# Attention with a top-1 expert layer on one core: zero writes moved into the attention, and a re-drawn plan

## The chip, the cores and the metric

The kernel runs on one core of one Trainium2 chip. The time is the device time of one execution in microseconds (us). The kernel before was timed three times: 327.14, 327.40 and 329.66 us, with a median of 327.4 us. Lower is better. The core has a matrix engine (PE, with its weight loads shown as PEld), a vector engine (DVE), a scalar engine (ACT), GpSimd (POOL), and SyncE (SP), which here only issues transfers. The transfers themselves run on 16 DMA engines.

## The reference, cut to what matters

```python
# q, k, v: (8 batches, 8 heads, 576 positions, 64), float32
scores = scale * q @ k.T                      # heads 0-3: local mask, heads 4-7: strided mask
attn   = softmax(where(mask, scores, -1e9))
x      = (attn @ v) as 4608 tokens x 512
logits = x @ w_gate                           # 8 experts
expert_idx, gate_w = argmax and softmax value of the logits
out    = zeros(4608, 512)
for e in range(8):                            # w1[e]: 512 x 1024, w2[e]: 1024 x 512
    tok = the 80 (capacity) tokens of expert e with the largest gate_w
    out[tok] = gate_w[tok] * (relu(x[tok] @ w1[e]) @ w2[e])
```

At most 640 of the 4608 rows of `out` are not zero. All 9.4 MB of `out` must still be written with zeros, and all 33.5 MB of expert weights must be read.

## The kernel before, in words

**Three stages.** (1) The attention, batch by batch in 32 steps (four per batch: two for the local heads, two for the strided heads). Its result is turned into token rows that are written to a scratch tensor `xs` in HBM, and into logits and gates. (2) The routing: the largest 16 gates per segment, their ranks, the slot of every kept token, and a gather of the kept rows from `xs` (`gather`, L1070). (3) The experts: 16 halves (w1 or w2 of one expert), 96 matmuls of 128x80 each, and a scatter of 80 rows of `out` per expert (L1173).

**Weights.** A half is four chunks of 512 KB, so there are 64 chunks. `wload` (L260) puts a chunk into a staging slot. ACT or POOL makes the high fp16 part (`high`, L268 or L270), then DVE makes the low part (L757 in the attention, L278 behind it). In the attention there are two staging slots (`ring`). From chunk 20 on there are eight: the two of `ring`, four pieces of `raw` and two pieces of `kst`; `raw` and `kst` hold q, k and transposed k during the attention. Split halves lie in `spl`: five buffers in the attention, eight afterwards.

**Zeros.** `zero_out` (L777) writes 512 KB of zeros from a 128 x 256 piece of `raw` called `zt`, so a packet has 1024 bytes. There are 18 of these writes.

**What sets the order.** In the attention an operation is put into a list with a priority, an engine (or two to choose from), a cost and its dependencies (`Plan.add`). `Plan.order` then walks through a model of the machine: at each step it takes the operation that can start first, ties within `SLACK` go by priority, and for transfers it keeps the time at which the DMA engines will be free. The sorted start times are the program order on every engine, and engines execute in that order. Weights and zeros are `bg` operations: they are taken only when the modelled transfer backlog is below `BGT`. Zeros are also `drop`: what has not been placed when the last steps begin is issued behind the attention (`pl.dropped`, L980). `lag` marks operations that may fall behind the others. Behind the attention the order is written out by hand: `rows_left` copies the last token rows, and `weave` mixes the halves, the splits and the scatters.

**Transfers.** All of them but the gathers and scatters are issued on SP, in program order. Each also waits for the transfer that was issued eight places before it on SP, because there are eight completion semaphores (DMAHW0 to 7).

Of the kernel before, what the change touches and what calls it, by code (L numbers as in the profile page):

```python
# [20 lines left out]
P = 128  # L21
# [37 lines left out]
class Plan:  # L59
# [6 lines left out]
    def add(self, prio, eng, cost, fn, rd=(), wr=(), mode=None, take=(), size=0, bg=False, after=(), lag=False, drop=False):  # L66
# [18 lines left out]
        self.ops.append(o)  # L85

    def order(self):
# [3 lines left out]
        dma, mode, fills = 0.0, None, []  # L91
        users, cand = {}, {e: [] for e in free}
# [7 lines left out]
        for _ in self.ops:  # L100
# [26 lines left out]
            if e == "T" and t - free["T"] > FGAP and (t < FILL0 or low > FILL1):  # L127
                i = min((i for i in range(nb) if held[i] is None), key=lambda i: bt[i], default=None)
                if i is not None and bt[i] < t - FGAP:
                    f, m = Op(), int((t - max(free["T"], bt[i]) - FGAP / 2) / C_FILL)  # L130
                    f.start, f.on, f.seq, f.fn = max(free["T"], bt[i]), "T", o.seq, lambda e, i=i, m=m: self.filler(i, m)
                    f.mode, f.cost, f.deps, f.take, f.size = 128, m * C_FILL, [], (), 0
# [34 lines left out]
def moe_attention(ctx: ExitStack, tc, q, k, v, wg, w1, w2, cap, out):  # L167
# [50 lines left out]
    outv = out.rearrange("(g p r) (h f) -> g p (r h) f", p=P, r=2, h=2)  # L218
# [152 lines left out]

    def do_load(l):

        b, g, w = l // 4, l // 2 % 2, l % 2
        src, t = (q, k)[w], raws[l % 3]
# [7 lines left out]
        add(l - QAH, "S", C_DMA, fn, wr=[raw_(l % 3)], size=560)  # L383
# [14 lines left out]
    def do_transposes(l):  # L398
        g, w = l // 2 % 2, l % 2
        i = cps[w] if g == 0 else raws[l % 3].rearrange("p u f -> p (u f)").rearrange("p (j f) -> p j f", f=P)  # L400
# [8 lines left out]
        for j3 in range(3):  # L409
# [7 lines left out]
            add(pr, "T", C_TR * 3, fill, rd=[CPS[w][j3] if g == 0 else raw_(l % 3)], wr=[x], take=[x], mode=128,  # L417
                after=[((("qt", j3), ("qs", j3))[g]) if w == 0 else ((("ktl", u, j3), ("kst", u, j3))[g]) for u in range(len(dvs))])
            for u, d in enumerate(dvs):
# [3 lines left out]
                add(pr + E_EV, "AV", c_copy(384, 0.1), ev, rd=[x],  # L423
# [43 lines left out]
    def do_scores(j):  # L467
# [67 lines left out]
        add(pj(j) + E_SUM, "V", (0.66 if g == 0 else 0.9) + 1.07e-3 * nt * nk, total, rd=PN, wr=[("sm", j % NPB)])  # L535
# [14 lines left out]
    def do_values(j):  # L550
# [6 lines left out]
        if g == 0:  # L557
            t0 = TL[it][0]
            for a, (c0, c1) in enumerate(TG[it]):
# [7 lines left out]
                for u in range(2):  # L567
                    add(pj(j) + E_PT + E_EV, "AV", c_copy(P * n, -0.03), lambda e, x=x, c0=c0, c1=c1, n=n, u=u: copy(
# [20 lines left out]
        else:  # L589
# [12 lines left out]
            for z0 in (0, 2):  # L602
# [10 lines left out]
                add(pj(j) + E_PT + E_EV, "AV", dict(A=0.86, V=0.7), ev, rd=[x], wr=[("pts", z0)])  # L613
# [72 lines left out]
    def do_logits(b):  # L686
# [5 lines left out]
        add(pr + 0.3, "A", 0.41, lambda e: nc.scalar.copy(lt, cols(x, 288)), rd=[x], wr=["lt"])  # L692
# [53 lines left out]
    def do_weights(i):  # L746
# [3 lines left out]
        if i >= NCH * NPRE:  # L750
            nm = [[("ring", 0)], [("ring", 1)], [raw_(0)], KST, KST][i - NCH * NPRE]
        pr = W0 + i * WSTEP
        add(pr - WAH, "S", C_DMA, lambda e: wload(i), wr=nm, size=524, bg=True)
        if i < NCH * NPRE:
            sn = ("spl", i // NCH)
            add(pr, "PA", dict(P=1.1, A=1.06), lambda e: high(e, hi, r), rd=nm, wr=[("hi", i)], lag=True)
            add(pr + 0.2, "V", 1.35, lambda e: nc.vector.scalar_tensor_tensor(lo, r, SC, hi, op0=ALU.mult,  # L757
# [18 lines left out]
    def zero_out(nz):  # L776
        nc.sync.dma_start(outv[nz], zt.unsqueeze(1).broadcast_to([P, 4, 256]))  # L777

    def do_constants():
# [54 lines left out]
    for l in range(3):  # L834
        do_load(l)
    do_constants()
    nr = 0
    for i in range(n + 2):
        if i == 0:
            for l in range(2):  # L840
                do_interleave(l)
                do_transposes(l)
                do_load(l + 3)
# [38 lines left out]
        if i == n + 1:  # L882
# [3 lines left out]
            add(pj(n - 1) + 4.4, "V", 0.25, lambda e, x=x: nc.vector.tensor_copy(g288[:, 2], cols(x, NQ)), rd=[x])  # L886
# [11 lines left out]
    nc.vector.memset(zt, 0.0)  # L898
# [448 lines left out]
```

## Time and profile before

| | |
|---|---|
| median of 3 runs | 327.4 us |
| the profiled execution, its own time | 326.44 us |
| its span, first to last instruction | 324.7 us |
| attention, to about | 205 us |
| last token rows and routing, to the first transpose of gathered rows | 229.60 us |
| experts, to the last matmul of a half | about 317 us |
| last scatters, to the end | 324.7 us |
| busy: PE, DVE, ACT, POOL | 266.4, 232.6, 224.9, 143.2 us |
| moved by DMA | 84.27 MB, mean 260 GB/s |

The profile cuts the span into 40 slices of 8.1 us and gives the busy share of each engine in tenths. Its answers by stretch of time give busy microseconds, the granted PE clock, the busy share of the DMA engines (which reads a little above 1 when they are full, since packets overlap) and the GB/s moved. Behind the attention a matmul of 128x80 is shown with a duration near 200 ns, but such matmuls are pipelined: counting how many are in a stretch says more than their busy time.

### The profile page before, as it was taken

To read this page: it belongs to the slowest core of one execution; us is meant where nothing else is said; L and a number is where in the kernel's file an instruction comes from. 1 tells how busy PE (TensorE), PEld (TensorE's weight loads), DVE (VectorE), ACT (ScalarE), POOL (GpSimd) and SP (SyncE) were. 2 spreads that over 40 slices of the span, in tenths; PEclk is the share of its full clock that TensorE was granted. 3 is DMA by queue.
4 is the path that set the end of the run, shared out by engine and by line. 5 is a ranking of instruction groups with operands and counts; after the bars stand their busy time and mean duration, and the time that the engine had idled before them with its cause. 6 is when DMAs were issued, how large, how long until landed. Compare 5 with 4: busy or idle time off the path is not lost. (4 is left out here: it accounts for less than half of the span.)

```text
span 324.7 us, 12775 instructions
## 1 busy us (share of the span) xinstructions
PE 266.4 (82%) x5408; PEld 236.0 (73%) x5408; DVE 232.6 (72%) x481; ACT 224.9 (69%) x440; POOL 143.2 (44%) x161
## 2 busy tenths in 40 slices
PE   7889799998998869986979889995670798789791
PEld 7788588777877758875758667885570797789791
DVE  7647588988897974876988974397320998779860
ACT  1569479896887587987888957680310998779751
POOL 8569754961753760474673860054410061111002
PEclk9999799999999997999999999997596599999997
DMA  7998868899799985888985998499999999998701
GB/s 248 197 334 261 216 200 226 224 313 245 216 244 268 278 246 176 226 253 225 261 222 137 273 226 310 133 275 333 372 360 342 402 392 377 393 351 283 272 24 46
DMA packets 56433, 84.27 MB, mean 260 GB/s; under 512 B 23346, under 2 KB 32564, under 8 KB 56372
## 3 DMA queue, kind: packets, MB, share of 16 engines
q1 hardware_dynamic: 55348, 80.79, 82.3%
q0 software_dynamic: 1024, 2.62, 2.3%
q8 instruction: 44, 0.72, 0.9%
q14 instruction: 17, 0.14, 0.1%
HBM read 63.21 MB, written 20.19 MB: 257 GB/s over the span
## 5 line engine op out<-in xcount | busy, mean ns | idle before, releaser
L1128 PEld LDWEIGHTS <-spl 128*128 128x128 f16 x512 | 52.9, 103 | 13.9 <-issue 13.7
L1129 PEld LDWEIGHTS <-spl 128*128 128x128 f16 x512 | 52.8, 103 | 5.0 <-issue 5.0
L1127 PEld LDWEIGHTS <-spl 128*128 128x128 f16 x512 | 52.9, 103 | 3.1 <-issue 3.1
L536 POOL TENSOR_TENSOR pb<-pb,sm 128x288 f32<-128x288 f32 (+2 forms) x32 | 37.9, 1183 | 34.1 <-DVE sm L534 23.7
L444 POOL TENSOR_SCALAR vlo<-vlo 32x1152 f32<-32x1152 f32 (+1 forms) x32 | 37.9, 1183 | 9.4 <-DMA vlo<-v 6.3
L1127 PE MATMUL yp<-he,spl 128*128 128x80 f16 x256 | 31.2, 208 | 11.1 <-ACT he L1142 10.9
L278 DVE SCALAR_TENSOR_TENSOR spl<-raw,spl 128x1024 f16<-128x1024 f32 x21 | 25.3, 1219 | 17.3 <-ACT spl L268 17.2
L1127 PE MATMUL hp<-xe,spl 128*128 128x80 f16 x256 | 31.3, 206 | 3.7 <-issue 2.7
L1128 PE MATMUL yp<-he,spl 128*128 128x80 f16 x256 | 31.1, 208 | 2.5 <-issue 1.4
L1129 PE MATMUL hp<-xe,spl 128*128 128x80 f16 x256 | 31.2, 206 | 1.4 <-issue 1.4
L268 ACT ACTIVATE spl<-raw 128x1024 f16<-128x1024 f32 x21 | 21.7, 1052 | 15.1 <-DMA raw<-moe_w 15.1
L1129 PE MATMUL yp<-he,spl 128*128 128x80 f16 x256 | 31.1, 208 | 1.0 <-issue 1.0
L1128 PE MATMUL hp<-xe,spl 128*128 128x80 f16 x256 | 31.2, 206 | 0.5 <-DVE xe L1122 0.3
L1173 POOL DMA_INDIRECT out<-ys,ids x8 | 9.2, 1154 | 48.0 <-ACT ys L1172 40.9
L529 ACT ACTIVATE pb<-pb 128x288 f32<-128x288 f32 (+2 forms) x32 | 18.2, 569 | 16.3 <-DVE pb L522 16.2
L757 DVE SCALAR_TENSOR_TENSOR spl<-ring,spl 128x1024 f16<-128x1024 f32 x20 | 25.9, 1297 | 4.3 <-POOL spl L270 3.6
L343 ACT COPY ktl<-bank 64x384 f32<-64x384 f32 (+1 forms) x47 | 25.9, 567 | 3.8 <-DVE ktl L347 2.4
L520 DVE TENSOR_REDUCE mx<-bank 128x16 f32<-128x288 f32 (+3 forms) x40 | 20.1, 502 | 11.4 <-PE bank L514 6.5
L532 DVE TENSOR_REDUCE sm<-pb 128x16 f32<-128x288 f32 (+2 forms) x32 | 22.8, 713 | 5.2 <-ACT pb L529 5.1
L581 PE MATMUL bank<-ptl,vlo 128*64 128x64 f32 x576 | 21.5, 227 | 5.9 <-issue 5.0
L1070 POOL DMA_INDIRECT xg<-xs,idx x8 | 10.6, 1324 | 33.8 <-DMA raw<-moe_w 21.4
L611 ACT ACTIVATE pts<-bank,hm 72x288 f32<-72x288 f32 x52 | 22.1, 497 | 4.6 <-DVE pts L605 2.7
(205 smaller groups left out, 751.1 us busy)
## 6 DMA issues: line engine op xcount, KB each, us to landing
ring<-moe_w SPq DMA_DIRECT2D x32, 512.0 KB
raw<-moe_w SPq DMA_DIRECT2D x21, 512.0 KB
raw<-q SPq DMA_DIRECT2D x16, 576.0 KB
raw<-k SPq DMA_DIRECT2D x16, 576.0 KB
out<-raw SPq DMA_DIRECT2D x18, 512.0 KB
kst<-moe_w SPq DMA_DIRECT2D x11, 512.0 KB
xs<-xn SPq DMA_DIRECT2D x12, 384.0 KB
vs<-v SPq DMA_DIRECT2D x8, 512.0 KB
```

The costliest lines, as they stand in the source:

```text
L268: nc.scalar.activation(hi, r, AF.Copy, scale=SC)
L278: nc.vector.scalar_tensor_tensor(lo, r, SC, hi, op0=ALU.mult, op1=ALU.subtract)
L343: nc.scalar.copy(o, i)
L444: add(4 * b + m + 0.6 + 0.4 * u, "P", 1.25 if m == 0 else 1.1, lambda e: nc.gpsimd.tensor_scalar(vlo[64 * u:64 * u + 32, t0:t1], vlo[64 * ...
L532: nc.vector.tensor_reduce(each(sm[:, 0:nt], g), pq, op=ALU.add, axis=AX.X)
L536: add(pj(j) + E_MUL, "P", 0.2 + 1.7e-3 * nt * nk, lambda e: nc.gpsimd.tensor_tensor(plain(pa, g), plain(pa, g), spread(sm[:, 0:nt], g), op ...
L581: nc.tensor.matmul(o[64 * h:64 * h + 64, :, k0:k0 + 32], vlo[:, 2 * (t0 + c0 + c) + p, h], ptl[:, c0 + c, :, 32 * gg:32 * gg + 32], start= ...
L611: nc.scalar.activation(pts[:, z].rearrange("p g h c -> p (g h) c"), tv(x), AF.Copy, scale=hm[0:72, z:z + 1])
L757: add(pr + 0.2, "V", 1.35, lambda e: nc.vector.scalar_tensor_tensor(lo, r, SC, hi, op0=ALU.mult, op1=ALU.subtract), rd=nm + [("hi", i)], l ...
L1127: nc.tensor.matmul(o, w[:, 0, i:i + P], x[:, 0, c], start=first, stop=False)
L1128: nc.tensor.matmul(o, w[:, 0, i:i + P], x[:, 1, c], start=False, stop=False)
L1129: nc.tensor.matmul(o, w[:, 1, i:i + P], x[:, 0, c], start=False, stop=last)
```

## The change

The diff does five things.

1. **Zero writes.** The 18 writes of 512 KB become 9 writes of 1 MB. The source is a 64 x 1024 piece of the `kst` tile that is zero throughout the attention (the part of the block-diagonal k for the other half of the partitions). A packet has 4096 bytes, and the source has 64 partitions where it had 128. A load of weights into `kst` must wait for the write.
2. **The plan's model.** The transfer model gets a start latency (`DSTART`), a shorter end latency and a higher rate. Consumers of a transfer get a margin (`SMARGIN`, and `LMARGIN` for operations with `lag`), other operations a smaller one. Costs of copies and splits are changed. The backlog up to which background transfers are taken rises from 0.3 to 3 us.
3. **A drawn plan.** Each priority gets a random part below 0.3 from a fixed seed.
4. **The fourth load** (k of the strided heads of batch 0) goes to a buffer of its own (`xt`), so that it need not wait for a free piece of `raw`.
5. **Late operations.** Planned `lag` operations that start behind the last gates are issued behind the first part of the routing, together with the zeros that are left.

```diff
         dma, mode, fills = 0.0, None, []
+        rng = random.Random(SEED)
+        for o in self.ops:
+            o.prio += SPREAD * rng.random()
...
             if o.size:
-                dma = max(dma, t + c) + o.size / DRATE + DGAP
+                dma = max(dma + DGAP, t + c + DSTART) + o.size / DRATE
                 o.done = dma + DLAT
...
-                u.ready = max(u.ready, o.done + (0 if u.eng == e else MARGIN if u.eng == "T" else HOP))
+                m = 0 if u.eng == e else MARGIN if u.eng == "T" else HOP
+                if e == "S" and u.eng != e:
+                    m = LMARGIN if u.lag else SMARGIN
+                u.ready = max(u.ready, o.done + m)
...
-    outv = out.rearrange("(g p r) (h f) -> g p (r h) f", p=P, r=2, h=2)
+    outv = out.rearrange("(g p r c) f -> g p r (c f)", p=64, r=4, c=2)
...
-    zt = raw[:, 6 * S:6 * S + 256]
+    zt = kstt[0:64, 4 * S // 2:4 * S // 2 + 1024]
...
+    def raw_of(l):
+
+        if l == 3:
+            return xts_[0][1].rearrange("p (u f) -> p u f", u=2), [("xt", 0, 1, a) for a in range(4)]
+        return raws[l % 3], [raw_(l % 3)]
...
-            nm = [[("ring", 0)], [("ring", 1)], [raw_(0)], KST, KST][i - NCH * NPRE]
+            nm = [[("ring", 0)], [("ring", 1)], [raw_(0)], KST + ["kstz"], KST + ["kstz"]][i - NCH * NPRE]
...
     def zero_out(nz):
-        nc.sync.dma_start(outv[nz], zt.unsqueeze(1).broadcast_to([P, 4, 256]))
+        nc.sync.dma_start(outv[nz], zt.unsqueeze(1).broadcast_to([64, 4, 1024]))
...
-        for nz in range(18):
-            add(50 + nz, "S", C_DMA, lambda e, nz=nz: zero_out(nz), size=544, bg=True, drop=True)
+        for nz in range(9):
+            add(50 + nz, "S", C_DMA, lambda e, nz=nz: zero_out(nz), rd=["kstz"], size=1010, bg=True, drop=True)
...
+    late_ops = []
     for o in pl.order():
-        o.fn(o.on)
+        if o.start > final.start and o.lag:
+            late_ops.append(o)
+        else:
+            o.fn(o.on)
...
-    for o in pl.dropped:
-        o.fn("S")
+    for o in late_ops + pl.dropped:
+        o.fn(o.on)
...
-DRATE = 370.0
+DRATE = 390.0
-BGT = 0.3
+BGT = 3
```

In the program orders below a row is an instruction on one engine. `ring0` and `ring1` (121, 122), `raw` (123) and `kst` (124) are staging memory, `spl_129` is the fifth half of the split weights.

**SP at the end of the attention and behind it.** Before, the transfers of token rows (L724) are followed by 16 zero writes (L777) and then by loads of weights (L260):

```order
L724 DMA xs<-vlo 96x1024 x2
L724 DMA xs<-ktl 96x1024 x2
L777 DMA out<-raw 512x1x256 x16
L260 DMA raw<-moe_w 128x2x512 x3
L260 DMA ring_121<-moe_w 128x1024
L260 DMA ring_122<-moe_w 128x1024
```

In the changed kernel the same place reads (L741 token rows, L794 zeros, L270 weights):

```order
L741 DMA xs<-vlo 96x1024 x2
L741 DMA xs<-ktl 96x1024 x2
L270 DMA ring_122<-moe_w 128x1024
L794 DMA out<-kst 256x1x1024
L270 DMA kst<-moe_w 128x1024
L270 DMA kst<-moe_w 128x2x512
L270 DMA raw<-moe_w 128x2x512 x3
L270 DMA ring_121<-moe_w 128x1024
```

One zero write is left there instead of 16. Three loads of weights that stood ahead of the last rows or among them (chunks 21, 23 and 24) now stand behind them.

**SP in the last quarter of the attention.** Before, the first of two zero writes here (L777) stands among loads of v (L432) and of weights (L260):

```order
L260 DMA ring_121<-moe_w 128x2x512
L432 DMA vlo<-v 32x10x64 x2
L777 DMA out<-raw 512x1x256
L432 DMA vlo<-v 32x10x64 x2
L432 DMA vlo<-v 32x8x64 x2
L260 DMA ring_122<-moe_w 128x2x512
```

In the changed kernel four zero writes stand in this quarter, the first two of them (L794) one load of v (L449) apart:

```order
L455 DMA vs<-v 64x4x512
L794 DMA out<-kst 256x1x1024
L449 DMA vlo<-v 32x10x64
L794 DMA out<-kst 256x1x1024
L449 DMA vlo<-v 32x10x64
L270 DMA ring_122<-moe_w 128x1024
L449 DMA vlo<-v 32x8x64
```

The kernel before has two smaller ones in that quarter and none earlier; the changed kernel has four more earlier, the first behind the first two loads of weights.

**DVE at the beginning of the routing.** Before, the ranks (L1015, L1017) follow directly on the indices of the largest gates (L975, L976):

```order
L968 TENSOR_TENSOR wgt<-cvi,segm 128x256
L975 MAX_INDEX cvi<-cvi,g_116 128x8
L976 MAX_INDEX cvi<-cvi,qs 128x8
L1015 TENSOR_SCALAR pos<-cvi 128x16
L1017 TENSOR_SCALAR scr,rank<-call,cvi 128x256 x3
L1020 SCALAR_TENSOR_TENSOR hit<-rank,capv,pos 128x3
```

In the changed kernel a split of weights (L774) stands between them:

```order
L990 TENSOR_TENSOR wgt<-cvi,segm 128x256
L997 MAX_INDEX cvi<-cvi,g_116 128x8
L998 MAX_INDEX cvi<-cvi,qs 128x8
L774 SCALAR_TENSOR_TENSOR spl_129<-ring_122,spl_129 128x1024
L1037 TENSOR_SCALAR pos<-cvi 128x16
L1039 TENSOR_SCALAR scr,rank<-call,cvi 128x256 x3
L1042 SCALAR_TENSOR_TENSOR hit<-rank,capv,pos 128x3
```

That split is chunk 19, the only late operation that is a split. It needs the high part from ACT, and on ACT that part (L278) stands behind the last copies of token rows (L353):

```order
L353 COPY ktl<-bank_149 96x2x256
L353 COPY ktl<-bank_150 96x2x256
L353 COPY ktl<-bank_151 96x2x256
L278 ACTIVATE spl_129<-ring_122 128x1024
L278 ACTIVATE spl_3610<-ring_121 128x1024
L278 ACTIVATE spl_3610<-ring_122 128x1024
```

Before, ACT goes from these copies (L343) straight to chunks 20 and 21 (`spl_3629` there is the sixth half):

```order
L343 COPY ktl<-bank_149 96x2x256
L343 COPY ktl<-bank_150 96x2x256
L343 COPY ktl<-bank_151 96x2x256
L268 ACTIVATE spl_3629<-ring_121 128x1024
L268 ACTIVATE spl_3629<-ring_122 128x1024
```

So the split of chunk 19 has moved from the attention into the routing, on both engines.

More of the change, by code (lines that the diff above doesn't have):

```diff
@@ L1 @@
-import itertools
+import random
 from contextlib import ExitStack
@@ L85, in add @@
         self.ops.append(o)
+        return o
     def order(self):
@@ L131, in order @@
                     f.start, f.on, f.seq, f.fn = max(free["T"], bt[i]), "T", o.seq, lambda e, i=i, m=m: self.filler(i, m)
-                    f.mode, f.cost, f.deps, f.take, f.size = 128, m * C_FILL, [], (), 0
+                    f.mode, f.cost, f.deps, f.take, f.size, f.lag = 128, m * C_FILL, [], (), 0, False
                     fills.append(f)
@@ L138, in order @@
                 c, mode = c + SWITCH, o.mode
+            c *= CF
             for x in o.take:
@@ L382, in fn @@
                                   src[b, 4:8].rearrange("h (p j) d -> (h p) (j d)", j=18))
-        add(l - QAH, "S", C_DMA, fn, wr=[raw_(l % 3)], size=560)
+        add(l - QAH, "S", C_DMA, fn, wr=nm, size=560)
     def do_interleave(l):
@@ L399, in do_transposes @@
         g, w = l // 2 % 2, l % 2
-        i = cps[w] if g == 0 else raws[l % 3].rearrange("p u f -> p (u f)").rearrange("p (j f) -> p j f", f=P)
+        rw, nm = raw_of(l)
+        i = cps[w] if g == 0 else rw.rearrange("p u f -> p (u f)").rearrange("p (j f) -> p j f", f=P)
         if w == 0:
@@ L416, in do_transposes @@
             pr = l - 2 + 0.25 * j3
-            add(pr, "T", C_TR * 3, fill, rd=[CPS[w][j3] if g == 0 else raw_(l % 3)], wr=[x], take=[x], mode=128,
+            add(pr, "T", C_TR * 3, fill, rd=[CPS[w][j3]] if g == 0 else nm, wr=[x], take=[x], mode=128,
                 after=[((("qt", j3), ("qs", j3))[g]) if w == 0 else ((("ktl", u, j3), ("kst", u, j3))[g]) for u in range(len(dvs))])
@@ L534, in total @@
             nc.vector.reciprocal(sm[:, 0:nt], sm[:, 0:nt])
-        add(pj(j) + E_SUM, "V", (0.66 if g == 0 else 0.9) + 1.07e-3 * nt * nk, total, rd=PN, wr=[("sm", j % NPB)])
+        add(pj(j) + E_SUM, "V", (0.6 if g == 0 else 0.8) + 1.07e-3 * nt * nk, total, rd=PN, wr=[("sm", j % NPB)])
         add(pj(j) + E_MUL, "P", 0.2 + 1.7e-3 * nt * nk, lambda e: nc.gpsimd.tensor_tensor(
@@ L755, in do_weights @@
             sn = ("spl", i // NCH)
-            add(pr, "PA", dict(P=1.1, A=1.06), lambda e: high(e, hi, r), rd=nm, wr=[("hi", i)], lag=True)
-            add(pr + 0.2, "V", 1.35, lambda e: nc.vector.scalar_tensor_tensor(lo, r, SC, hi, op0=ALU.mult,
+            add(pr, "PA", dict(P=1.06, A=0.96), lambda e: high(e, hi, r), rd=nm, wr=[("hi", i)], lag=True)
+            add(pr + 0.2, "V", 1.14, lambda e: nc.vector.scalar_tensor_tensor(lo, r, SC, hi, op0=ALU.mult,
                                                                               op1=ALU.subtract), rd=nm + [("hi", i)], lag=True)
@@ L833, in moe_attention @@
     n = 4 * B
-    for l in range(3):
+    for l in range(4):
         do_load(l)
@@ L842, in moe_attention @@
                 do_transposes(l)
-                do_load(l + 3)
+                if l:
+                    do_load(l + 3)
             for m in range(2):
@@ L897, in moe_attention @@
     nc.vector.memset(wgt, 0.0)
-    nc.vector.memset(zt, 0.0)
     nc.vector.tensor_copy(mloc[:, 0], mloc[:, 1])
@@ L1289 @@
 FREE0 = dict(T=5.0, A=2.5, V=5.2, P=7.0, S=0.8)
-HOP = 0.1
-MARGIN = 0.5
+HOP = 0.15
+CF = 1.0
+SEED, SPREAD = 99245, .3
+MARGIN = .2
+SMARGIN = 1.0
+LMARGIN = 3.0
 TLAT = 0.2
 SWITCH = 0.11
-DRATE = 370.0
+DRATE = 390.0
 DGAP = 0.2
-DLAT = 1.8
+DSTART = 1.7
+DLAT = 1.2
 C_DMA = 0.5
@@ L1299 @@
 PEN = 1.5
-AHEAD = 6
+AHEAD = 5
 LASTB, LASTN = 3, 2
 FGAP, FILL0, FILL1, C_FILL = 0.6, 40, 28, 0.0556
-SLACK = 0.01
-BGT = 0.3
+SLACK = .05
+BGT = 3
 E_EV = 0.1
@@ L1307 @@
 E_MX = 0.3
-E_EXP = 0.6
+E_EXP = .4
 E_SUM = 0.9
-E_MUL = 1.0
-E_PT = 1.6
+E_MUL = .8
+E_PT = 1
 E_O = 0.2
@@ L1314 @@
 VAH = ((2, 2), (3,))
-W0, WSTEP, WAH = 3, 1, 2
+W0, WSTEP, WAH = 3, 1.2, 2
 LASTP = 29
-VPEN = 0.4
+VPEN = .4
 RC0 = 4
@@ L1320 @@
 XP0, XPS = 0.3, 0.6
-XQ0, XQS = 0, 0.2
+XQ0, XQS = 0, .2
 _INS = ['q', 'k', 'v', 'moe_w_gate', 'moe_w1', 'moe_w2']
```

16 lines of the change are left out of this document (8 added, 8 removed).

## The prediction, made before the changed kernel was run

> **What bounds the kernel now.** I read the page's slices first, then busy time by stage, then SP's timeline and the waits behind the attention. The slices: PE, the DMA engines and what they moved.
>
> ```profile
> PE   7889799998998869986979889995670798789791
> DMA  7998868899799985888985998499999999998701
> GB/s 248 197 334 261 216 200 226 224 313 245 216 244 268 278 246 176 226 253 225 261 222 137 273 226 310 133 275 333 372 360 342 402 392 377 393 351 283 272 24 46
> ```
>
> PE is near 9 in the attention (25 slices), and falls to 0 in one slice at 243 to 251 us while the DMA engines are full. By stage (columns: stretch, length, busy us and count of PE, PEld, DVE, ACT and POOL, PE clock, DMA share, GB/s):
>
> ```profile
> 0.00:205.00 205.00, 180.35 (x3583) 153.64 (x3584) 157.05 (x352) 155.88 (x338) 118.78 (x131) 0.98 0.86 239
> 217.60:229.60 12.00, 5.91 (x76) 5.35 (x74) 7.93 (x25) 1.49 (x2) 6.80 (x7) 0.80 1.03 335
> 229.60:316.40 86.80, 66.62 (x1579) 64.83 (x1580) 58.84 (x66) 57.13 (x80) 12.91 (x11) 0.89 0.90 325
> 229.60:240.60 11.00, 10.12 (x202) 9.73 (x203) 4.97 (x6) 4.04 (x6) 2.91 (x4) 0.75 1.06 371
> 240.60:252.00 11.40, 0.84 (x19) 0.61 (x16) 0.00 (x0) 0.91 (x1) 0.00 (x0) 0.70 1.03 348
> 264.00:288.00 24.00, 19.39 (x502) 18.90 (x500) 20.16 (x22) 18.35 (x27) 4.66 (x3) 1.00 1.03 385
> 292.00:304.00 12.00, 10.88 (x287) 10.63 (x284) 11.56 (x14) 10.64 (x15) 0.92 (x1) 1.00 0.92 305
> ```
>
> The expert stage is 86.8 us, for 58.8 us of DVE work. For 11.4 us almost nothing runs. What is moved then, by SP's timeline (start, duration, transfers):
>
> ```profile
> 216.25 1.29 SPq L724 DMA_DIRECT2D xs<-ktl  x2
> 217.59 24.56 SPq L777 DMA_DIRECT2D out<-raw  x16
> 242.25 6.56 SPq L260 DMA_DIRECT2D raw<-moe_w  x3
> ```
>
> Sixteen zero writes hold SP for 24.56 us and the next weights are issued only at 242.25. Who waits for them (total, times, longest):
>
> ```profile
> ACT spl L268 <- DMA raw<-moe_w: 15.1, 2, 14.8
> PE yp L1127 <- ACT he L1142: 10.9, 1, 10.9
> ```
>
> ACT waits 14.8 us for weights; PE's 10.9 us hang on the relu queued behind that split. So the attention is set by PE and its neighbours, and the expert stage by zeros ahead of weights, then until 288 by the weights themselves (DMA share 1.03).
>
> **The burst goes (gain).** Only one of these writes remains ahead of the weights. The load of chunk 24 waits for it, since it overwrites its source; the loads behind wait too. At the transfer price below that is some 5 us, against 24.56. The experts then run ahead on staged chunks, so DVE sets the pace: from 292 to 304 it is busy 11.56 of 12 us while 287 PE records pass, 23.9 per us. All 1579 records at that pace take 66.1 us. One cold start remains: 202 records in the 11.0 us to 240.6 are 8.4 us of work at the same pace, so 2.6 us more. 66.1 + 2.6 = 68.7 us in place of 86.8: **-18.1**. Bounds: DVE's 58.84 us at 96% busy plus the start, 63.7 us (-23.1); the pace of 264 to 288, 502 / 24 = 20.9 per us, 75.5 us (-11.3). What is late next is the split on DVE, not the load: the 40 chunks from 24 on, at 512 KB / 385 GB/s = 1.36 us each, are 54 us, less than 68.7.
>
> **The late split (loss).** The rows of the routing, by the timeline:
>
> ```profile
> 213.27 0.45 DVE L976 FIND_INDEX8 cvi<-cvi,qs 128x8 uint32<-128x288 f32 x1
> 213.83 0.17 DVE L1015 TENSOR_SCALAR pos<-cvi 128x16 f32<-128x16 f32 x1
> 215.15 2.05 ACT L343 COPY ktl<-bank 96x512 f32<-96x512 f32 x4
> 217.06 2.04 ACT L268 ACTIVATE spl<-ring 128x1024 f16<-128x1024 f32 x2
> 222.61 0.17 DVE L1065 TENSOR_REDUCE idx<-tab 80x8 int32<-80x16 f32 x1 [0.81 <-PE tab L1056]
> 222.89 1.22 DVE L278 SCALAR_TENSOR_TENSOR spl<-ring,spl 128x1024 f16<-128x1024 f32 x1
> 223.22 1.98 POOL L1070 DMA_INDIRECT xg<-xs,idx  x1 [4.20 <-DMA out<-raw]
> 229.60 0.77 PE L1119 MATMUL xp<-ident,xg 80*128 80x80 f32 x4 [3.97 <-DMA xg<-xs,idx]
> ```
>
> Now the low part of chunk 19 stands on DVE ahead of L1015 and waits for its high part, which ACT can begin only behind the row copies, at 217.06. High part 1.02 (half of 2.04), low part 1.22: L1015 begins at about 219.3 in place of 213.83, **+5.5**. All that is queued behind it on DVE moves with it: ranks, slots, the indices at 222.61, and through them the gather on POOL and the first transpose on PE at 229.60. Its cover was the attention: before, DVE sat idle there late, as the row for its next work shows.
>
> ```profile
> 207.72 0.35 DVE L651 TENSOR_REDUCE lg<-bank 96x48 f32<-96x192 f32 x1 [6.11 <-PE bank L648]
> ```
>
> SP's load of chunk 21 waits for the same split, so the weights start near 219.5; that is inside the slack above. Bounds: the gather lands 6.4 us after its issue beside a full queue and may land up to 2 us sooner beside the wait for the zero write (+3.5). The longest split of the attention took 2.08 us, by the row of L757 (shortest, median and longest in ns), which would make it +6.4.
>
> ```profile
> L757 DVE SCALAR_TENSOR_TENSOR spl<-ring,spl x20: 1160/1214/2082, 29.4 to 191.0; 128x1024 f16<-128x1024 f32 x20
> ```
>
> **Eight zero writes in the attention (loss).** Their price is not in the trace as such. The nearest rows are stretches in which one kind of transfer is alone:
>
> ```profile
> 118.50:119.50 1.00, 0.56 (x19) 0.43 (x16) 0.16 (x1) 0.99 (x4) 1.00 (x2) 1.00 1.07 201
> 142.00:144.00 2.00, 2.00 (x90) 1.66 (x79) 0.96 (x3) 1.19 (x3) 1.77 (x2) 1.00 1.01 381
> 144.50:146.50 2.00, 2.00 (x60) 1.70 (x60) 1.52 (x3) 1.94 (x5) 1.19 (x1) 1.00 1.05 179
> 210.50:212.50 2.00, 1.96 (x17) 1.65 (x15) 1.77 (x6) 1.18 (x3) 0.00 (x0) 1.00 0.98 281
> 219.00:241.00 22.00, 14.97 (x257) 14.01 (x256) 11.50 (x29) 4.13 (x7) 8.39 (x9) 0.77 1.05 354
> ```
>
> What SP issued just ahead of the first three:
>
> ```profile
> 113.86 1.47 SPq L438 DMA_DIRECT2D vs<-v  x2
> 139.14 0.39 SPq L379 DMA_DIRECT2D raw<-q  x1
> 139.61 0.43 SPq L260 DMA_DIRECT2D ring<-moe_w  x1
> 140.90 1.15 SPq L438 DMA_DIRECT2D vs<-v  x2
> ```
>
> At 142 to 144 a q load and a weight chunk, both to 128 partitions, move at 381 GB/s. Behind them, at 144.5 and again at 118.5, the load of `vs` to 64 partitions fills the engines too (1.05, 1.07) but moves 179 and 201 GB/s. Token rows from 96 partitions move 281. The new writes read 64 partitions, so I take 201 GB/s: 1.049 MB / 201 = 5.2 us each. Ends: 381 GB/s, 2.75 us; 179 GB/s, 5.9 us.
>
> [...]
>
> Eight at 5.2 are 41.7 us of full engines. Away go two small writes (2 x 0.524 MB / 354 = 3.0) and three chunks (3 x 1.36 = 4.1): net +34.6, with ends +15 and +40. The engines have, at 0.86 of 1.03, 34 us free in these 205 us. So the attention would need them nearly always full. They need not be late for that: `raw` has room for three loads of q and k, and in the loaded stretch below nothing is lost.
>
> ```profile
> 60.00:120.00 60.00, 54.53 (x1130) 45.76 (x1127) 50.83 (x111) 48.61 (x108) 35.76 (x30) 1.00 0.94 257
> POOL vlo L444 <- DMA vlo<-v: 6.3, 2, 4.4
> POOL cp L395 <- DMA raw<-k: 3.9, 2, 2.1
> ```
>
> Here the share is 0.94 (91% of full) for 60 us with PE busy 54.5, 91%, above its 88% mean. Transfers held up POOL by 6.3 and 3.9 us. At 91% the attention would take 205 / 0.91 = 225 us (+20), at 100% 205 (0). I take 97%, **+6**, because a queue with a 5 us write in it seldom runs dry.
>
> **The rest.** The fourth load in its own buffer, the costs and the random part only re-order work on engines that keep their counts. PE is idle for 24.7 of these 205 us, so a better order could give some; a worse one, with margins of 1 and 3 us for transfers that now come later than modelled, could take some: 0, within -4 to +4. Writing 9 MB in 9 issues in place of 18 saves SP time only where SP is behind, which it is not once the burst is gone.
>
> **Sum.** -18.1 + 5.5 + 6 = -6.6. The profiled execution took 326.44 us (span 324.7), which makes 319.8; the median of the runs is 1.0 above it, so 327.4 - 6.6 = **320.8 us**.
>
> **Rivals.**
> - *The writes run at full rate* (24%): for it, the small writes ran at 354 GB/s with packets a quarter as long; against it, the rows for 64 and 96 partitions. Then +15 us of transfer lie in the 34 free ones, the attention stays at 205, and the sum is -12.6: 314.8; with a better order (-4), 311.
> - *The attention becomes transfer-bound* (18%), the slower side: the place is SP's queue from the first zero write on, the mechanism 5.2 us at the head of the queue eight times, where loads behind it are needed at once. For it: the sum leaves no idle time, and the model that made the order holds such a write for 2.6 us (1010 / 390). Against it: loads are issued steps ahead. At 91% full, +20, the sum is +7.4: 334.8. It decides from +12.6 on; above +15.9 the kernel is slower by 1%.
> - *The experts stay at the pace of the loads* (12%): 75.5 us in place of 68.7, if staging slots come free as late as before. For it, loads on SP wait for splits also now; against it, until 288 the DMA engines were full, so slots were not the limit. Sum -11.3 + 5.5 + 6 = +0.2: 327.6; with less in the attention, 322.
> - *My forecast* (46%). That the zeros are not moved is excluded by SP's order.
>
> **How the numbers follow.** A measurement of this kernel can tell about 1% (3.3 us) from no change. Forecast: 38 of its 46 points lie below 324.1, 8 within 1%. Full rate: 24 faster. Transfer-bound: 5 within, 13 slower. Pace of the loads: 3 faster, 8 within, 1 slower. Together 0.65, 0.21, 0.14. The range runs from full rate with the larger gain behind (-23.1 + 3.5 = -19.6: 308) to short of the transfer-bound case, 331; outside are some 2 in 10.
>
> **What would show it.** Right: no stretch of 10 us with PE idle behind the attention; L1037 on DVE starts some 5 us behind L998; a zero write fills the engines at near 200 GB/s; the first gathered transpose about 11 us later than 229.6; experts in 66 to 71 us. Wrong: a zero write at 350 GB/s or more; an attention beyond 218 us; experts at 75 us with DVE waiting for ACT and ACT for weights.

## The result, and the profile after

The changed kernel took 320.8 us (median of 4 runs, 317.6 to 322.9) against 328.4 us for the kernel before beside it (327.1 to 329.7). The ratio is 0.969, 95% interval 0.960 to 0.978: faster. Executions of one program spread by 1 to 4% here, and ratios and intervals compare only those near the fastest of each kernel. The median forecast was 320.8 us. That it was hit this closely is no merit of the terms, as will be seen: the attention was wrong by 8 us, and the routing and the experts by 3 us each in the other direction.

The profiled execution took 317.6 us (span 315.9). Its page, the same three lines of the slices as before (PE, the DMA engines, what they moved):

```profile
PE   7997987998898899895979987967259969988891
DMA  7999999899998799995789999689999999899501
GB/s 246 217 267 377 252 226 323 260 298 264 334 273 250 202 286 285 317 237 205 199 239 247 215 239 345 210 257 283 270 264 336 338 384 377 288 407 389 193 25 48
```

The zero of PE at 243 us is gone. A dip remains at 221 to 237 us (slices 29 and 30), in the routing. The stages in the table of stretches (stretch, length, busy us and count of PE, PEld, DVE, ACT and POOL, PE clock, DMA share, GB/s):

```profile
0.00:205.00 205.00, 182.95 (x3626) 156.69 (x3627) 166.25 (x359) 154.84 (x334) 112.62 (x126) 0.98 0.95 262
...
211.50:235.95 24.45, 11.13 (x123) 10.31 (x124) 11.59 (x43) 7.99 (x13) 9.93 (x18) 0.86 0.91 274
235.95:307.40 71.45, 63.97 (x1574) 62.69 (x1575) 58.82 (x66) 56.71 (x80) 10.85 (x11) 0.95 0.87 308
250.00:300.00 50.00, 43.49 (x1118) 42.67 (x1115) 42.54 (x48) 40.84 (x59) 6.03 (x6) 1.00 0.94 339
```

| stage, us | before | after | difference | forecast |
|---|---|---|---|---|
| attention, to the end of the last index | 213.7 | 211.5 | -2.2 | +6 |
| routing, to the first gathered transpose | 15.9 | 24.45 | +8.6 | +5.5 |
| experts, to just short of the last matmul of a half | 86.8 | 71.45 | -15.3 | -18.1 |
| rest | 8.3 | 8.5 | +0.2 | 0 |
| span | 324.7 | 315.9 | -8.8 | -6.6 |

The routing in the timelines of VectorE, ScalarE, POOL and TensorE, put in order of time:

```profile
211.05 0.45 DVE L998 FIND_INDEX8 cvi<-cvi,qs 128x8 uint32<-128x288 f32 x1
213.10 1.07 ACT L353 COPY ktl<-bank 96x512 f32<-96x512 f32 x2 [3.06 <-DMA xs<-ktl]
218.86 2.03 ACT L278 ACTIVATE spl<-ring 128x1024 f16<-128x1024 f32 x2
219.99 1.22 DVE L774 SCALAR_TENSOR_TENSOR spl<-ring,spl 128x1024 f16<-128x1024 f32 x1 [8.49 <-ACT spl L278]
221.13 0.17 DVE L1037 TENSOR_SCALAR pos<-cvi 128x16 f32<-128x16 f32 x1
229.30 2.03 POOL L1092 DMA_INDIRECT xg<-xs,idx  x1 [12.52 <-DMA kst<-moe_w]
235.95 0.73 PE L1141 MATMUL xp<-ident,xg 80*128 80x80 f32 x4 [3.65 <-DMA xg<-xs,idx]
```

VectorE stands still for 8.49 us: the low part of chunk 19 waits for its high part, and that stands on ScalarE behind row copies. These were themselves held up for 3.06 us, because the buffer `ktl` was still being written out to `xs`. (In the row of the gather, L1092, the transfer named last is not the condition that matters; what the gather waits for is worked out below.) Behind the routing, SP's timeline shows one zero write in place of sixteen:

```profile
218.06 1.29 SPq L741 DMA_DIRECT2D xs<-ktl  x2
221.24 0.36 SPq L270 DMA_DIRECT2D ring<-moe_w  x1
221.65 0.54 SPq L794 DMA_DIRECT2D out<-kst  x1
222.28 7.24 SPq L270 DMA_DIRECT2D kst<-moe_w  x2
```

### The profile page after: what moved, and what is told of

It is laid out like the page before. It is cut to its first block, busy times and chain, and to the rows that moved or that the text cites. A ratio compares the mean times of both kernels' runs of the same rounds, so it can differ in the third digit from the quotient of the medians.

```text
span 315.9 us, 12765 instructions
## 1 busy us (share of the span) xinstructions
PE 265.2 (84%) x5399; PEld 235.3 (74%) x5399; DVE 242.4 (77%) x487; ACT 225.3 (71%) x438; POOL 135.2 (43%) x156
## 3 DMA queue, kind: packets, MB, share of 16 engines
q0 software_dynamic: 1024, 2.62, 2.6%
## 5 line engine op out<-in xcount | busy, mean ns | idle before, releaser
L553 POOL TENSOR_TENSOR pb<-pb,sm 128x288 f32<-128x288 f32 (+2 forms) x32 | 34.9, 1092 | 61.1 <-DVE sm L551 44.3
L1150 PEld LDWEIGHTS <-spl 128*128 128x128 f16 x512 | 52.1, 102 | 3.7 <-issue 3.6
L1149 PEld LDWEIGHTS <-spl 128*128 128x128 f16 x512 | 52.1, 102 | 3.0 <-issue 3.0
L1151 PEld LDWEIGHTS <-spl 128*128 128x128 f16 x512 | 52.1, 102 | 2.1 <-issue 2.1
L774 DVE SCALAR_TENSOR_TENSOR spl<-ring,spl 128x1024 f16<-128x1024 f32 x20 | 28.3, 1424 | 9.4 <-ACT spl L278 9.4
L1149 PE MATMUL hp<-xe,spl 128*128 128x80 f16 x256 | 31.7, 208 | 3.4 <-issue 2.8
L1150 PE MATMUL hp<-xe,spl 128*128 128x80 f16 x256 | 31.6, 207 | 1.4 <-issue 1.1
L1151 PE MATMUL hp<-xe,spl 128*128 128x80 f16 x256 | 31.6, 208 | 0.0
L353 ACT COPY ktl<-bank 64x384 f32<-64x384 f32 (+1 forms) x49 | 26.4, 566 | 4.8 <-DMA xs<-ktl 3.1
L1149 PE MATMUL yp<-he,spl 128*128 128x80 f16 x256 | 28.8, 202 | 1.2 <-issue 1.2
L1150 PE MATMUL yp<-he,spl 128*128 128x80 f16 x256 | 28.8, 202 | 1.1 <-issue 1.1
L1151 PE MATMUL yp<-he,spl 128*128 128x80 f16 x256 | 28.8, 202 | 0.4 <-issue 0.3
L1195 POOL DMA_INDIRECT out<-ys,ids x8 | 7.6, 950 | 50.1 <-ACT ys L1194 50.1
L598 PEld LDWEIGHTS bank<-ptl,vlo 128*64 128x64 f32 x576 | 19.5, 139 | 12.7 <-issue 10.6
L278 ACT ACTIVATE spl<-ring 128x1024 f16<-128x1024 f32 x23 | 23.8, 1057 | 4.5 <-DMA ring<-moe_w 4.5
L353 ACT COPY ptl<-bank 64x256 f32<-64x256 f32 (+2 forms) x46 | 21.3, 473 | 6.8 <-PE bank L581 3.4
L549 DVE TENSOR_REDUCE sm<-pb 128x16 f32<-128x288 f32 (+2 forms) x32 | 22.8, 711 | 3.7 <-ACT pb L546 3.7
L546 ACT ACTIVATE pb<-pb 128x288 f32<-128x288 f32 (+2 forms) x32 | 18.1, 565 | 9.9 <-DVE pb L539 9.7
L353 ACT COPY xt<-bank 128x288 f32<-128x288 f32 (+3 forms) x40 | 16.8, 441 | 11.0 <-PE bank L598 7.7
```

The costliest lines, as they stand in the source:

```text
L278: nc.scalar.activation(hi, r, AF.Copy, scale=SC)
L353: nc.scalar.copy(o, i)
L546: add(pj(j) + E_EXP, "A", 0.13 + 0.83e-3 * nt * nk, lambda e: nc.scalar.activation(pa, pa, AF.Exp), wr=PN)
L549: nc.vector.tensor_reduce(each(sm[:, 0:nt], g), pq, op=ALU.add, axis=AX.X)
L553: add(pj(j) + E_MUL, "P", 0.2 + 1.7e-3 * nt * nk, lambda e: nc.gpsimd.tensor_tensor(plain(pa, g), plain(pa, g), spread(sm[:, 0:nt], g), op ...
L598: nc.tensor.matmul(o[64 * h:64 * h + 64, :, k0:k0 + 32], vlo[:, 2 * (t0 + c0 + c) + p, h], ptl[:, c0 + c, :, 32 * gg:32 * gg + 32], start= ...
```

## The experiments

Each kernel is a variant of the changed one. Kernels of one group ran on one chip and share the runs of the kernel before: 326.9 us in the first group (after_again, split_in_place, split_in_place_zero_early, zeros_behind), 326.0 in the second (ladder, zeros_128, zeros_128_split_in_place, no_spread), 324.6 in the third (the rest). Ratios are to these.

**after_again**, no edit.

> The changed kernel unaltered, as the yardstick for the three others of this group. Both theories expect its stages as in its first profile: last index at 211.5 us, first gathered transpose at 236, end of the experts' matmuls at 307, and 0.97 of the time before.

322.5 us (317.0 to 328.3), ratio 0.975 (0.962 to 0.989). The spread is wide. The profiled execution is the longest, 328.3 us, and shows what a lower clock goes with. Of the first 200 us, this execution and then the changed kernel's first one:

```profile
0.00:200.00 200.00, 175.45 (x3415) 150.16 (x3416) 155.59 (x337) 145.07 (x310) 108.72 (x122) 0.93 0.95 256
```
```profile
0.00:200.00 200.00, 178.48 (x3569) 153.42 (x3569) 164.88 (x356) 151.68 (x327) 112.62 (x126) 0.98 0.96 265
```

At a granted clock of 0.93 the last index ended at 222.5 us, at 0.98 at 211.5, 11 us earlier. The two kernels with added transfers at their end (`ladder` and `ladder_pairs` below) have the same attention, and there it ended at 216.3 us at 0.95 and at 213.1 at 0.97. If the starts of the same VectorE instructions are compared one by one, after_again lags behind the changed kernel's first execution by 2.5 us from 60 to 100 us, by 4.1 from 121 to 131, by 6.8 from 139 to 148 and by 10.4 at 199. The lag steps up at 52, 104, 134 and 189 to 202 us, just where the clock of after_again was halved for 3.4 or 6.8 us. So the clock is what made this attention longer; what halves it, the traces do not show. Attentions are compared below only between executions at about the same clock, and since each is a single execution, differences of less than about 2 us between them mean little.

**zeros_behind**: what does moving the zeros bring, and what the new plan?

```
-        if o.start > final.start and o.lag:
+        if getattr(o, "drop", False) or o.start > final.start and o.lag:
             late_ops.append(o)
```

> The changed kernel with the same plan, but all nine zero writes issued together behind the indices, none inside the attention. It tells what moving the zeros brings from what the new plan brings. Theory 'zeros': the attention was not made longer by eight 1 MB writes, so the last index stays at 211.5 (within 1 us); nine writes of 2.6 us, 23 us of transfers, stand ahead of the loads of chunks 23 on, of which the 14 us until the first gathered transpose hide a part; the experts take 80 to 87 us and the time is 9 to 16 us above the changed kernel's. Rival 'plan': the gain came from the other order of the attention and the weights; then the last index is as in the changed kernel too, but the time is within 3 us of it. Theory 'half rate' of the prediction: without the writes of 5.2 us each the attention gets 6 us shorter (last index at 205).

349.7 us, ratio 1.070 (1.062 to 1.078). Its last index, two stretches, and the two longest waits for the weights behind it:

```profile
207.41 0.45 DVE L998 FIND_INDEX8 cvi<-cvi,qs 128x8 uint32<-128x288 f32 x1
```
```profile
0.00:200.00 200.00, 180.55 (x3617) 154.79 (x3617) 165.59 (x356) 153.57 (x332) 111.64 (x126) 0.98 0.82 227
...
243.00:259.00 16.00, 0.00 (x0) 0.00 (x0) 0.00 (x0) 0.00 (x0) 0.00 (x0) 0.50 1.00 213
```
```profile
ACT spl L278 <- DMA ring<-moe_w: 45.4, 1, 45.4
DVE spl L288 <- ACT spl L278: 34.8, 1, 34.8
```

Three things follow. First, at the same clock (0.98) and with the same plan but no zeros, the attention ends at 207.9, against 213.7 before: all that the diff does there besides the zero writes is worth -5.9 us. That is the new order, and also two small zero writes, three loads of weights and one split that are no longer in the attention; no run parts these.

Second, with the eight zero writes the attention ends 3.6 us later, at 211.5, between the 0 and the 6 us of the text's theories. By the starts of the same VectorE instructions, the changed kernel lags behind zeros_behind by 0.7 us at 100 us, by nothing at 145, and by 3.6 from 173 us to the end; around its last two writes (184.87, 187.58) the lag does not grow. Each execution also has two stretches of 3.4 us at half clock, at 147 and 164 us here and at 146 and 180 there. So whether all of the 3.6 us is the writes' is not shown. What they take of the DMA engines can be read as well: the share of the first 200 us rises from 0.82 to 0.96, that is by 28 us, an estimate of 3.5 us a write.

Third, behind the attention these writes have the engines to themselves, with a share of 1.00 at only 213 GB/s, and the weights wait behind them. The price was expected at 9 to 16 us over the changed kernel; by the two ratios (1.070 and 0.975 for after_again) it is 31, since at 213 GB/s a write takes 4.9 us, nearly twice the 2.6 us assumed there.

**ladder** and **ladder_pairs**: the price of a write by itself, and of two side by side (both kernels carry extra transfers at their end, so their times mean nothing).

```
...
+        for n, p0 in ((128, 0), (64, 0), (64, 64), (32, 0)):
+            r = 256 // n
+            for hf in range(2):
+                nc.sync.dma_start(sd[256 * hf:256 * hf + 256].rearrange("(p r) f -> p r f", r=r),
+                                  sb[p0:p0 + n, 0:1024].unsqueeze(1).broadcast_to([n, r, 1024]))
...
```

> The changed kernel with sixteen more transfers behind its last step, 1 MB each in 4096-byte packets, in pairs, each pair waiting for the one before: writes from 128 partitions, from partitions 0 to 63, from 64 to 127, from 0 to 31; then loads into 0 to 63, 128, 64 to 127, 128 and 0 to 31. Theory 'half rate': by itself a write from 64 partitions moves about 200 GB/s (5.2 us for 1 MB) and one from 128 about 380 (2.8 us), from 32 about 100; loads alike. Rival 'full rate' (as the windows of the changed kernel read where such writes ran beside other transfers, 370 to 430 GB/s): all writes take 2.6 to 2.8 us, and only the loads differ. The added work costs some 110 us behind the last step; only its own rows count.

> The changed kernel with 1 MB transfers behind its last step, this time side by side: writes from partitions 0 to 63 beside writes from 64 to 127; writes from 0 to 63 beside loads into all 128; beside loads into 0 to 63; and loads into 0 to 63 beside loads into 64 to 127 (writes from all 128 stand between the groups). The first ladder showed 200 GB/s for 64 partitions alone and about 400 for 128. Theory 'halves': each half of the partitions has its own 200 GB/s, and another transfer can use the other half; then the two halves side by side move 380 to 420 together, a half beside 128 partitions 300 to 400, and two on the same half 200. Rival 'engines': a transfer from 64 partitions holds all engines at half speed; then every group stays at 200 to 300. By the first, the attention's windows of 370 to 430 GB/s with such a write in them are understood, and the write's price there is below 5.2 us.

Stretches of the ladder: writes from 128 partitions, from 0 to 63, from 64 to 127, from 0 to 31, then loads into 0 to 63 and into 128. Below, of the pairs, writes from both halves side by side:

```profile
332.50:335.50 3.00, 0.00 (x0) 0.00 (x0) 0.00 (x0) 0.00 (x0) 0.00 (x0) 0.50 1.02 404
337.00:347.00 10.00, 0.00 (x0) 0.00 (x0) 0.00 (x0) 0.00 (x0) 0.00 (x0) 0.50 1.00 208
349.00:355.00 6.00, 0.00 (x0) 0.00 (x0) 0.00 (x0) 0.00 (x0) 0.00 (x0) 0.50 1.01 205
360.00:364.00 4.00, 0.00 (x0) 0.00 (x0) 0.00 (x0) 0.00 (x0) 0.00 (x0) 0.50 0.99 199
372.00:378.00 6.00, 0.00 (x0) 0.00 (x0) 0.00 (x0) 0.00 (x0) 0.00 (x0) 0.50 0.94 190
380.00:382.00 2.00, 0.00 (x0) 0.00 (x0) 0.00 (x0) 0.00 (x0) 0.00 (x0) 0.50 0.99 410
```
```profile
336.00:354.00 18.00, 0.00 (x0) 0.00 (x0) 0.00 (x0) 0.00 (x0) 0.00 (x0) 0.50 1.00 240
```

A 64-partition write by itself runs at half the rate of 128 partitions, 208 or 205 GB/s against 404: 1.049 MB / 208 = 5.0 us, from either half. 32 partitions are hardly slower than 64 (199), where the text had expected about 100. Why 32 and 64 move at one rate, half that of 128, no run here shows. Two halves one behind the other in one queue move 240 GB/s at a share of 1.00, far from the 380 to 420 of the theory 'halves', which falls: here such a write holds all engines. The other three groups of ladder_pairs, writes beside loads and two loads, moved anywhere from 158 to 465 GB/s in stretches of 2 us, and are not read here.

In the attention it is neither always so nor never. Two stretches of the changed kernel, with other transfers in them too: behind the write issued at 171.29, and behind those issued at 184.87 and 187.58:

```profile
173.50:177.00 3.50, 3.50 (x106) 3.12 (x107) 3.33 (x9) 3.50 (x11) 1.99 (x2) 1.00 1.00 204
189.00:193.00 4.00, 2.61 (x48) 2.10 (x46) 3.93 (x6) 2.54 (x6) 3.75 (x4) 1.00 1.02 376
```

Packet by packet: in the ladder a 4096-byte packet takes near 160 ns in the 128-partition writes and 325 ns in the 64-partition ones (16 full engines at 404 and 208 GB/s give 162 and 315). Counted in the traces between 20 and 210 us, packets of 4096 bytes that took more than 315 and less than 335 ns:

```
before 77    zeros_128 78    after 522    split_in_place 557    no_spread 728
```

Eight writes are 2048 packets; 522 - 78 = 444, about a fifth, ran at half rate. Of all packets of this size that began in the two stretches above, 158 of 173 took 315 to 335 ns in the first, and 223 of 251 took 140 to 180 ns in the second. What decides which, no run here settles.

**zeros_128**: the same bytes at the same places from all partitions.

```
+    zt2 = raw[:, 6 * S:6 * S + 256]
...
-        nc.sync.dma_start(outv[nz], zt.unsqueeze(1).broadcast_to([64, 4, 1024]))
+        for m in range(2):
+            nc.sync.dma_start(outw[2 * nz + m], zt2.unsqueeze(1).broadcast_to([P, 4, 256]))
```

> Every zero write of 1 MB from 64 partitions in 4096-byte packets is made as two of 512 KB from 128 partitions in 1024-byte packets, at the same places. Theory 'half rate': what lengthens and scatters the attention is that a write occupies half of the engines for 5.2 us; spread over all it takes 2.75 us, the last index comes at 208 to 209 us as with the zeros behind, and the time is 3 to 8 us below the changed kernel's, 0.95 to 0.965 of the time before. Rival 'bytes': only the bytes count; everything as in the changed kernel, 0.97 to 0.975. Rival 'packets': four times the packets take longer; the attention's last index is at 215 to 225 and the time is that of before.

319.9 us, ratio 0.979 (0.966 to 0.993). Its last index and its first 200 us:

```profile
212.26 0.45 DVE L1002 FIND_INDEX8 cvi<-cvi,qs 128x8 uint32<-128x288 f32 x1
```
```profile
0.00:200.00 200.00, 177.22 (x3559) 151.53 (x3560) 163.81 (x355) 151.40 (x326) 112.51 (x126) 0.98 0.92 264
```

The clock is 0.98 again, and the last index ends at 212.7, where 208 to 209 would have shown the half rate at work. The DMA engines do have less to do: against zeros_behind (0.82) the share rises by 20 us and not by 28, an estimate of 2.5 us a write in place of 3.5. But this is time that the engines had to spare, so a fifth of the packets at half rate cannot be seen in the end of the attention. 'Bytes' is the nearest of the three theories, and 'packets' falls. Four more kernels below have zeros from 128 partitions; at a clock of 0.97 or 0.98 their last index ends at 210.5 to 215.5 us, on both sides of the 213.1 that 0.97 gives with zeros from 64.

**split_in_place**, and the same with zeros from 128 partitions, **zeros_128_split_in_place**: the split of chunk 19 where the planner had put it, only SP's load kept behind.

```
-        if o.start > final.start and o.lag:
+        if o.start > final.start and o.lag and o.on == "S":
```

> Chunk 19's split (ScalarE and VectorE) is emitted at the place the planner gave it, ahead of the first MAX8, and only the load of chunk 21 is kept behind the indices. Theory 'routing': VectorE's idle 8.5 us behind the last index was the price of the late split, and the first gathered transpose sets when the end comes; the last index then moves from 211.5 to about 212.7 (one more 1.2 us operation ahead of it), the first gathered transpose from 236 to 228, and the end by the same 8 us, to 0.975 of the changed kernel's time. Rival 'stream': the weights' transfers, nearly without a gap from 210 to 297, set the end of the experts; then the gathered transpose is still 8 us earlier, the experts take 69 to 79 us instead of 71.5, and the time falls by 0 to 2 us only (0.995).

> Both: zero writes from 128 partitions, and chunk 19's split at its planned place. If the late split and the half rate are separate prices they add: the kernel with the split in place stood at 317.5 us against 322.5 for the changed one, so 3 to 5 us below the kernel with zeros from 128 partitions alone, about 310 to 314. If the stream of weights sets the end, the gain is 0 to 2 us over the better of the two.

317.5 us (316.3 to 318.4), ratio 0.971 (0.964 to 0.978), and 315.4 us (313.6 to 317.7), ratio 0.970 (0.957 to 0.982). By the ratios that is 1.5 and 3.1 us below the same kernel with the late split on the same chip (after_again, zeros_128). The intervals overlap, so the gain in time is not shown; what follows rests on the profiles. From split_in_place, VectorE and TensorE:

```profile
209.10 1.22 DVE L774 SCALAR_TENSOR_TENSOR spl<-ring,spl 128x1024 f16<-128x1024 f32 x1
212.62 0.45 DVE L998 FIND_INDEX8 cvi<-cvi,qs 128x8 uint32<-128x288 f32 x1
213.10 0.17 DVE L1037 TENSOR_SCALAR pos<-cvi 128x16 f32<-128x16 f32 x1
221.55 0.24 DVE L1070 SCALAR_TENSOR_TENSOR slot<-jc,small,sel 128x16 bf16<-128x16 f32 x1 [2.61 <-PE small L1065]
232.99 0.77 PE L1141 MATMUL xp<-ident,xg 80*128 80x80 f32 x4 [6.12 <-DMA xg<-xs,idx]
```

The idle 8.5 us are gone, and a new wait of 2.61 us is there: the routing's prefix matmuls stand on TensorE behind the last rows' transposes and 48 warming matmuls. But the first transpose is only 19.9 us behind the index, not 15. The next runs take away what is left on VectorE's and TensorE's chain.

**no_warm**, **low_part_behind**, **low_part_behind_no_warm** (all with zeros from 128 partitions):

The first edit below, on top of zeros_128_split_in_place, is that of no_warm; the second, on top of zeros_128, that of low_part_behind; the third kernel has both.

```
-WARM_ = [48, 0, 32, 0]
+WARM_ = [0, 0, 32, 0]
```
```
+        if o.start > final.start and o.lag and o.on in "SV":
...
     gather(0)
+    for o in late_ops + drp[1:]:
+        o.fn(o.on)
```

> zeros_128_split_in_place without the 48 warming matmuls that TensorE has queued ahead of the two matmuls of the routing's prefix (they do nothing but keep its clock up). There the slots waited 2.6 us for them. Theory: first gathered transpose 17 to 17.5 us behind the last index in place of 19.7, and the time falls by 2 to 2.5 us. Rival: the clock is lower for longer at the start of the experts, their stage takes 2 us more, and nothing is gained.

> Zeros from 128 partitions; chunk 19's high part at its planned place on ScalarE, its low part on VectorE behind the indices, and the loads of chunks 21 and 23 to 27 behind that (the ninth zeros ahead). Theory 'routing': the low part of 1.2 us leaves the chain to the gather, the gather meets fewer loads in the queue; first gathered transpose 16.5 to 18.5 us behind the last index in place of 19.7, time 1 to 3 us below zeros_128_split_in_place. Rival 'stream': the weights start 2 to 4 us later and the end comes by as much later.

> Both of the two before. If the two prices are separate they add: first gathered transpose 14.5 to 16.5 us behind the last index (before: 15.8), time 3 to 5 us below zeros_128_split_in_place, 309 to 313; if the experts then wait for weights, their stage takes 76 to 78 us in place of 74 and the gain is 1 to 2 us.

316.6 us (308.6 to 318.5, too wide for a ratio), 314.7 (0.970, 0.958 to 0.983) and 316.5 (0.978, 0.967 to 0.988). None is clearly better than zeros_128_split_in_place. The granted clock from 225 to 240 us was 0.66 in low_part_behind, which has the 48 warming matmuls, and 0.54 in low_part_behind_no_warm; from 240 to 300 it was 1.00 in both. The indices do come earlier, yet the first transpose hardly does. From the timelines of SP, VectorE, POOL and TensorE (us, counted from the end of the last index; "last rows issued" is the first of the last two writes of token rows, the second follows about 1 us later):

| kernel | last rows issued | indices | gather begins | gather behind last rows | gather behind indices | first transpose |
|---|---|---|---|---|---|---|
| before | 2.5 | 8.9 | 9.5 | 7.0 | 0.6 | 15.9 |
| after | 6.6 | 17.3 | 17.8 | 11.2 | 0.5 | 24.45 |
| zeros_128 | 6.8 | 17.6 | 18.1 | 11.2 | 0.5 | 26.7 |
| split_in_place | 5.4 | 10.9 | 12.0 | 6.6 | 1.1 | 19.9 |
| zeros_128_split_in_place | 5.9 | 10.8 | 13.0 | 7.0 | 2.1 | 19.6 |
| no_warm | 5.3 | 8.4 | 12.4 | 7.1 | 4.0 | 19.9 |
| low_part_behind | 6.0 | 11.8 | 12.8 | 6.8 | 1.0 | 21.4 |
| low_part_behind_no_warm | 6.3 | 9.3 | 12.6 | 6.3 | 3.3 | 20.6 |

In no kernel of this table does the gather begin sooner than 6.3 us behind the issue of the last rows, which it reads. In the kernel before, the gather began 7.0 us behind the rows and 0.6 behind the indices, so both conditions came close together. With the late split the indices are the later ones; once they come early, the rows are, and earlier indices only wait longer (4.0 us in no_warm). That the gather then waits for the landing of the rows is inferred from these times, as the profile's releasers do not name it. So the late split costs 11.2 - 7.0 = 4.2 us of the path, and the other 4.1 us of the longer routing are rows that come 6.6 us behind the index instead of 2.5. The first transposes agree: 24.45 us with the late split and 19.9 without, 4.5 us. The wait of 3.06 us for `ktl` shown above lies on the path of the rows; no run took it away alone.

**split_in_place_zero_early**: besides, the ninth zero write and the load of chunk 23 inside the attention.

```
...
+        if o is w19:
+            zlast.fn("S")
+            early.fn("S")
```

> As the one before, and besides the ninth zero write and the load of chunk 23 are issued right behind chunk 19's load (about 201 us), where the transfers were only 0.26 to 0.67 busy from 201 to 207, instead of behind all rows' writes at 222. Theory 'routing': no more than the kernel before (0 to 1 us). Rival 'stream': the stream of weights behind the attention carries about 4 us less (2.6 for 1 MB of zeros, 1.4 for one chunk), and the end comes 3 to 4 us sooner than in the kernel before. If the row writes wait for the two transfers instead, the first gathered transpose is 2 to 4 us later than there.

319.4 us (315.1 to 322.2), ratio 0.968 (0.956 to 0.981): no gain to be seen over split_in_place, 317.5. Of the text's cases the third came: the last rows were issued 8.1 us behind the index instead of 5.4, and the first transpose stood at 22.8 instead of 19.9. The attention, too, ended 3.1 us later at the same clock (216.2 and 213.1 us at 0.97). What was put ahead of the rows in SP's queue delayed the gather here: it began 15.4 us behind the index instead of 12.0.

**no_spread**: the drawn part of the priorities off.

```
-SEED, SPREAD = 99245, .3
+SEED, SPREAD = 99245, 0.0
```

> The changed kernel with the planner's random part of the priorities set to 0, all other numbers as they are. If the new order's gain in the attention (last index 5.8 us earlier than before when the zeros are behind) is that of the new costs and due times, the last index comes within 4 us of the changed kernel's 211.5 to 222.5; if it is that of the drawn order, the last index comes 5 to 10 us later than 222.

One execution, 325.1 us, last index at 218.8 with the clock at 0.97. By its words the text's first answer (the costs and due times) came, but its span, from 4 us below 211.5 to 4 above 222.5, is too wide to decide. Against the executions of the drawn order at 0.97 (split_in_place and ladder_pairs, both 213.1) it is 5.7 us late, about as much as the 5.9 us above. But this plan also puts all nine zero writes into the attention, the last two issued at 197.83, and a load of weights into `kst` at 212.63. So it is a hint that the drawn order mattered, not more.

## Why the prediction came out right

*The burst goes, -18.1.* Right in direction and cause, 2.8 us too large: -15.3. The step that failed is the pace. The prediction took 23.9 records per us, from a stretch with VectorE 96% busy, for the whole stage. In the changed kernel 1118 records pass in the 50 us from 250 to 300, 22.4 per us, and VectorE is 85% busy. The waits of SP and of the engines in the stage:

```profile
SPq L270 <- DVE spl L288: 34.5, 25, 5.2
```
```profile
DVE spl L288 <- ACT spl L278: 6.8, 7, 1.3
ACT y L1185 <- PE yp L1151: 5.0, 5, 1.8
```

Loads wait for splits, splits to a small part for ScalarE, and the DMA share is 0.94: no engine is full by itself. The rival 'pace of the loads' said 75.5 us, the forecast 68.7; 71.45 lies between, and which link sets the pace stays open. The stage hardly depended on when it began: from the first gathered transpose to the last output transpose it took 72.5 to 75.4 us in all variants with at most one zero write behind the attention.

*The late split, +5.5.* The mechanism is right: L774 waits 8.49 us and L1037 begins 9.6 us behind the index, where some 5 were said. By the table of the gather its price on the path is 4.2 us. What the prediction missed is that the row copies ahead of the split would end later: it took the time of the kernel before (217.06, 3.3 us behind the index there) for the time of the new one (218.86, 7.4 behind). That shift, +4.1 at the last rows' issue, was among 'the rest', at 0. Together +8.6, outside the bound of +6.4. The sign 'first gathered transpose about 11 us later' did not come: it was 6.35 us later, since the attention ended earlier and not later.

*The zero writes, +6.* The price of 5.2 us is right for a write by itself, 5.0 in the ladder. In the attention it was too high: about a fifth of the packets paid it, and the share of the engines rose by an estimated 3.5 us a write. Both signs, 'near 200 GB/s' and '350 or more', can be read there (204 and 376). The assumption that the engines would be 97% full failed too. Their share over 205 us is 0.95, which is 92% of the 1.03 that the prediction calls full. At 91% its own sum gives +20 us, so that sum, which lets the attention grow as the engines' share falls short of full, has no support here. The loss of the eight writes at equal clock was +3.6, between two single executions.

*The rest, 0 within -4 to +4.* With the zero writes' term this makes the largest miss, -2.2 in place of +6 for the attention. All that changed there besides the eight writes is worth -5.9 us. In it are the two small writes and three loads that the prediction had counted, as 7.1 us of transfers, under the zero writes. So -5.9 is not the new order alone, and whether the order lies outside the range stays open. The text had seen that TensorE was idle for 24.7 us there and gave it nothing.

*The rivals.* 'Full rate', with 2.75 us a write, was nearer to the 3.5 us than the forecast, and it named a better order as a further case, but it gave no place to the later rows; 'transfer-bound' did not come, the attention got shorter.

*The number.* Against its own profile the prediction said 319.8, and 317.6 came. The errors, -8.2 in the attention, +3.1 in the routing, +2.8 in the experts and +0.2 behind them, leave -2.1 (the sum of rounded stages). The median then lay 3.2 above the profiled execution, not 1.0, which made up for it. Counted from the kernel before beside it (328.4), the change is -7.6 us and not the -6.6 of the forecast. The burst and the late split were at work as named; for the attention the sign was wrong; the exact figure is an accident.

## What to carry to other kernels

Before pricing a step that is moved, list every condition of the instruction that waits behind it, here the indices and the token rows of one gather, and see which is second: taking away the later one gains only the distance to the other. What a transfer takes by itself was not its price in a mixed queue here: a write took 5.0 us by itself and an estimated 3.5 in the mix, and the nine writes put together behind the attention cost 31 us, where eight inside it cost 3.6 between two executions. And where a planner is re-tuned together with an edit, split the two by one run with the edit alone, at the same granted clock.

## What was not expected of the hardware

The granted TensorE clock over the first 200 us differed between executions of the same program, 0.98 and 0.93, with stretches of 3.4 or 6.8 us at half clock, and moved the end of the attention by 11 us, more than any edit tried inside it. And 64-partition writes ran partly at near 160 ns a packet and partly at 325 ns within one kernel, while the two halves of the partitions in one queue reached only 240 GB/s.
